# Strassen's algorithm for the first feed-forward product of seven token blocks, with the second product's weights streamed from DRAM

## The chip, the cores and the metric

The kernel runs on one core of a Trainium2 chip. The metric is the device time of one execution in microseconds (us). The core has a matrix engine (TensorE, here PE, with its weight loads listed as PEld), an elementwise engine (VectorE, DVE), an activation engine (ScalarE, ACT), a general engine (GpSimd, POOL), and SyncE (SP), which here only issues DMA transfers. Each engine works off its own instructions in order and waits on semaphores for the others. Matmuls write to PSUM, eight banks of 512 floats on each of 128 partitions; everything else lies in SBUF or in DRAM.

## The reference

Three stages run one after the other on 4608 tokens of 512 features: attention with pooled keys and values, a mixture of eight experts with one expert chosen per token, and a dense feed-forward stage with 2048 hidden features. The change concerns the last one:

```python
def _moe2_ref(x, w_in, w_out) -> np.ndarray:
    h = x @ w_in
    g = h * (1.0 / (1.0 + np.exp(-h)))
    return (g @ w_out).astype(np.float32)
```

x is 4608x512, w_in 512x2048, w_out 2048x512. The weights arrive as 64-bit floats.

## The kernel before

To keep the precision of float32, the kernel splits each operand of a large product into a high and a low part (`split`: ACT rounds the high part, DVE subtracts it) and adds three products, high x high, high x low and low x high.

The feed-forward stage (`ffn`) cuts the tokens into nine blocks of 512 (`ORDER`, last block first) and the hidden features into 16 blocks f of 128. A block's x is loaded (`load_x`), transposed on PE in four groups k of four 128x128 tiles (`xtrans`) and split into `xth` and `xtl`. The transposes go alternately to the PSUM tags "fxp" (one bank) and "hp" (three banks). For each f, `mm1` makes the first product, 12 matmuls of 512 columns (three split products x four slices of the 512 features) into one bank of "hp". ACT takes its sigmoid (`fsg`), DVE multiplies, ACT casts the high part (`fgh`), and DVE subtracts it (`fgl`). `mm2` makes the second product of f-1 meanwhile: 12 matmuls of 512 columns, which add onto four banks `fop0` to `fop3`, one for each 128 tokens of the block. So PE has mm1(f), mm2(f-1), mm1(f+1) and so on, and at a block's end mm2(15) with the next block's transposes between. `store` then copies the four banks out, the even ones on DVE and the odd ones on ACT, and SP sends them to DRAM.

The 16 weight pairs stay in SBUF all the time. They are converted from 64-bit floats (`ffn_ops`, `ffn_conv3`, steps taken from the generator `conv` inside `mm1`) while the first two blocks run. For that the first block is run in two visits, f 0 to 5 first and f 6 to 15 after the second block; the partial sums go to DRAM (`part`) between them and come back with `load_part`. So there are three visits, and then seven blocks that have nothing to convert.

All instructions of an engine keep the order in which the program writes them (`Ordered`): a copy that is written behind the steps of `conv` waits for them. The recorded line of almost every instruction is that helper's (L110), so the profile is read by tile names.

Of the kernel before, what the change touches and what calls it, by code (L numbers as in the profile page):

```python
# [5 lines left out]
F32 = mybir.dt.float32  # L6
F32R = mybir.dt.float32r
# [5 lines left out]
AF = mybir.ActivationFunctionType  # L13
ALU = mybir.AluOpType
# [4 lines left out]
P = 128  # L19
B, H, S, D = 8, 8, 576, 64  # L20
G = 72
NT = B * S
DM = H * D
# [129 lines left out]
class Kern:  # L153
# [931 lines left out]
    def ffn(self, xa, pool, dr):  # L1085
        nc, tc = self.nc, self.tc
        with tc.tile_pool(name="fs", bufs=1) as s1, \
# [61 lines left out]
            def store(b, ops, fs):  # L1149
# [9 lines left out]
                for s in range(4):  # L1159
                    o = s2.tile([P, DM], F32, name=f"fo{b}_{s}", tag="fo", bufs=4)  # L1160
                    if fs[0] > 0:
                        nc.vector.tensor_tensor(o, ops[s], self.part[s // 2][:, DM * (s % 2):DM * (s % 2 + 1)], ALU.add)
                    elif s % 2:
                        nc.scalar.copy(o, ops[s])
                    else:
                        nc.vector.tensor_copy(o, ops[s])
                    for bt, off, r, m in parts(4 * b + s):
                        nc.sync.dma_start(self.out[S * bt + off:S * bt + off + m, :], o[r:r + m, :])

            def load_part():  # L1170
                self.part = []
                for i in range(2):
                    t = mt[i]
                    nc.sync.dma_start(t.rearrange("p (s d) -> p s d", s=2),
                                      part[2 * i:2 * i + 2].rearrange("s p d -> p s d"))
                    self.part.append(t)


            self.ready = []

# [8 lines left out]
            def part_done(n):  # L1189
                if n + 1 < 16:  # L1190
                    self.ffn_abs(n + 1, *mt)
                self.ffn_conv3(n, pool)
                if n + 3 < 16:
                    self.ffn_load(n + 3)

            mt = [s1.tile([P, 2 * DM], F32, name=m, tag=m) for m in ("fm", "ft")]
            self.ffn_abs(NPRE, *mt)
# [5 lines left out]
            visits += [(b, range(16)) for b in ORDER[2:]]  # L1203
            for (b, fs), after in zip(visits, [v[0] for v in visits[1:]] + [None]):
                ops = [po.tile([P, DM], F32, name=f"fop{b}_{fs[0]}_{s}", tag=f"fop{s}") for s in range(4)]
                g = {}
                for f in fs:
                    g[f] = mm1(b, f, pace.pop(0) if pace else 2)
                    if f == fs[0] + 2 and after is not None:
                        load_x(after)  # L1210
                    if f == fs[0] + 4 and fs[0] > 0:
                        load_part()
                    if f == fs[-1] and after is not None:
                        xtrans(after, 0)
                        xtrans(after, 1)
                    if f > fs[0]:
                        mm2(f - 1, g.pop(f - 1), ops, fs)
                mm2(fs[-1], g.pop(fs[-1]), ops, fs, (lambda k: xtrans(after, k)) if after is not None else None)
                store(b, ops, fs)


def layout(q, k, v, w_skip, w_gate):
# [67 lines left out]
```

## Time and profile before

| | |
|---|---|
| median of 3 runs | 1363.56 us (1360.55 to 1364.36) |
| the profiled execution | 1363.74 us, its span 1362.0 us |
| PE busy | 1301.8 us, 96% of the span |
| PEld busy | 1111.8 us, 82% |
| DVE busy | 684.5 us, 50% |
| ACT busy | 502.9 us, 37% |
| POOL busy | 247.8 us, 18% |
| granted TensorE clock, mean | 0.987 |

The span runs from the first to the last instruction; 1.74 us of the execution lie around it. A group of instructions in the profile is named by what it writes and reads: "fh<-w1l,fh" is a matmul of the first product, "fop<-fh,fgh" one of the second. In a timeline each line has the start, the length of the whole run of equal instructions, and their number; what the engine waited for stands in brackets. A matmul's modelled end lies behind the next one's start, since matmuls overlap, so its pitch is read from starts.

### The profile page before, as it was taken

How to read it: one execution, taken by the hardware profiler on the slowest of the kernel's cores; microseconds unless marked ns; L12 is line 12 of the kernel's file. 1: busy time of each engine (PE TensorE's matmuls, PEld its weight loads, DVE VectorE, ACT ScalarE, POOL GpSimd, SP SyncE). 2: the span in 40 equal slices, each digit the busy share in tenths (PEclk: the TensorE clock that was granted, in tenths of full speed). 3: DMA queues.
4: the chain of work that ended last, by engine and by line, in shares of the span. 5: the costliest groups of instructions: out<-in, count | busy, mean ns of one | idle time of the engine just before them, and what ended most of it. 6: DMA issues, size and time to landing. Idle time of an engine off the chain costs nothing.

```text
span 1362.0 us, 19973 instructions
## 1 busy us (share of the span) xinstructions
PE 1301.8 (96%) x6645; PEld 1111.8 (82%) x6646; DVE 684.5 (50%) x1297; ACT 502.9 (37%) x1087; POOL 247.8 (18%) x216
## 2 busy tenths in 40 slices
PE   6899798999989998989999999999999999999998
PEld 5788687889978888878888888888888888888887
DVE  5777786766677766878523223232232232322322
ACT  4676534444455434354422223222232222322322
POOL 4466433322333431223200000000000000000000
PEclk9999998999989998999999999999999999999999
DMA  9998445555566542435021001001010010100000
GB/s 286 291 276 279 156 129 203 191 190 171 169 215 194 183 148 86 144 121 174 11 93 62 2 1 62 0 28 35 0 62 1 0 63 0 62 1 0 32 0 31
DMA packets 62997, 141.45 MB, mean 104 GB/s; under 512 B 11612, under 2 KB 21468, under 8 KB 60295
## 3 DMA queue, kind: packets, MB, share of 16 engines
q1 hardware_dynamic: 55631, 123.53, 28.0%
q0 software_dynamic: 7008, 16.80, 3.8%
q8 instruction: 43, 0.70, 0.2%
q10 hardware_dynamic: 288, 0.20, 0.1%
q14 instruction: 27, 0.22, 0.1%
HBM read 113.37 MB, written 29.82 MB: 105 GB/s over the span
## 4 chain that ended last, share of the span: by engine, by line
PE 58%; DVE 2%; issue 1%; ACT 0%; DVEq 0%; ACTq 0%
PE fop L110 28%; PE fh L110 28%; PE hp L110 1%; PE fxp L110 1%; DVE fr L110 1%; DVE ft L110 1%; PE yp L110 0%; DVE w1l L110 0%; ACT fm L110 0%; DVE fsg L110 0%; DVE fgl L110 0%; DVE raw L110 0%; ACT fh L110 0%; ACT fsg L110 0%; DVE x L110 0%
## 5 line engine op out<-in xcount | busy, mean ns | idle before, releaser
L110 DVE TENSOR_TENSOR fsg<-fh,fsg 128x512 f32<-128x512 f32 x144 | 99.6, 691 | 399.9 <-ACT fsg L110 399.9
L110 PE MATMUL fh<-w1l,fh 128*128 128x512 f32 x1008 | 248.9, 389 | 0.0
L110 ACT ACTIVATE fsg<-fh 128x512 f32<-128x512 f32 x144 | 86.3, 599 | 421.7 <-PE fh L110 421.6
L110 PEld LDWEIGHTS fh<-w1l,fh 128*128 128x128 f32 x1008 | 189.2, 188 | 39.5 <-DVE w1l L110 0.2
L110 PE MATMUL fop<-fh,fgh 128*128 128x512 f32 x504 | 199.2, 395 | 0.2 <-ACT fgh L110 0.2
L110 PE MATMUL fop<-fl,fgh 128*128 128x512 f32 x504 | 196.7, 390 | 0.0
L110 DVE TENSOR_TENSOR fgl<-fsg,fgh 128x512 fp32r<-128x512 f32 x144 | 99.7, 692 | 87.7 <-ACT fgh L110 87.4
L110 PE MATMUL fop<-fh,fgl 128*128 128x512 f32 x504 | 140.2, 390 | 1.6 <-DVE fgl L110 1.6
L110 ACT CAST fgh<-fsg 128x512 fp32r<-128x512 f32 x144 | 89.3, 620 | 123.4 <-DVE fsg L110 120.5
L110 PE MATMUL fh<-w1l,fl 128*128 128x512 f32 x504 | 134.7, 389 | 0.0
L110 PEld LDWEIGHTS fop<-fh,fgl 128*128 128x128 f32 x504 | 94.9, 188 | 21.9 <-DVE fgl L110 2.0
L110 PEld LDWEIGHTS fop<-fh,fgh 128*128 128x128 f32 x504 | 95.0, 189 | 19.3 <-ACT fgh L110 0.6
L110 PEld LDWEIGHTS fh<-w1l,fl 128*128 128x128 f32 x504 | 94.6, 188 | 19.6
L110 PEld LDWEIGHTS fop<-fl,fgh 128*128 128x128 f32 x504 | 95.0, 189 | 18.7
L110 PE MATMUL yp<-w2h,hh 128*128 128x512 f32 x240 | 96.8, 403 | 1.7 <-ACT w2h L110 1.7
L110 PE MATMUL yp<-w2l,hh 128*128 128x512 f32 x240 | 94.3, 393 | 2.2 <-DVE w2l L110 2.2
L110 PE MATMUL yp<-w2h,hl 128*128 128x512 f32 x240 | 94.7, 395 | 0.0
L110 ACT ACTIVATE hh<-hp 128x256 fp32r<-128x256 f32 (+2 forms) x96 | 41.2, 429 | 126.5 <-PE hp L110 119.6
L110 PE MATMUL hp<-xth,w1h 128*128 128x256 f32 (+2 forms) x384 | 73.7, 315 | 9.8 <-ACTq L943 5.9
L110 PE MATMUL hp<-xtl,w1h 128*128 128x256 f32 (+2 forms) x384 | 74.7, 313 | 7.2 <-DVE xtl L110 6.8
L110 ACT ACTIVATE prb<-s,mx 128x72 f32<-128x72 f32 x288 | 65.4, 344 | 43.2 <-DVE mx L110 43.2
L110 PE MATMUL hp<-xth,w1l 128*128 128x256 f32 (+2 forms) x384 | 71.7, 310 | 0.0
(181 smaller groups left out, 1885.9 us busy)
## 6 DMA issues: line engine op xcount, KB each, us to landing
raw<-w SPq DMA_DIRECT2D x88, 512.0 KB, 4.4
xa<-x SPq DMA_DIRECT2D x36, 256.0 KB, 5.0
fx<-xa SPq DMA_DIRECT2D x9, 1024.0 KB, 6.4
v<-vR SPq DMA_DIRECT2D x7, 1200.0 KB, 14.5
fr<-w_in SPq DMA_DIRECT2D x16, 512.0 KB, 4.4
fr<-w_out SPq DMA_DIRECT2D x16, 512.0 KB, 5.1
out<-fo SPq DMA_DIRECT2D x32, 256.0 KB, 2.4
k<-kT SPq DMA_DIRECT2D x7, 1152.0 KB, 10.0
```

What stands on the lines that cost most here:

```text
L110: ins = f(*a, **k)
```

## The change

The first two blocks stay as they are, in three visits. For the other seven, the first product is taken two hidden blocks at a time (a pair p, eight of them, called a slot here): x and the pair's 512x256 weights are both cut into 2x2 halves, and Strassen's algorithm in Winograd's form makes seven products of halves instead of eight. Each is three split products x two slices, so 42 matmuls of 256 columns a pair where there were 24 of 512. The seven products need sums of the halves of x (`xsum`, on DVE, from transposes `xt`, which ACT copies to SBUF), split like x, and sums of the halves of the weights. The latter are made once, by the generator `sums`, in the third visit (`SUMS` steps an f) and in the first slots of the first Strassen block. They overwrite the second product's weights in SBUF. Those were written to DRAM before (`keep_out`, on SP's queue) and are now streamed back for every block (`load_out`, on POOL's queue) into four buffers, used in turn.

A slot makes its products in four groups (`prods`), each into one bank of "hp": p1 and p6, p7 and p5, p4, p2 and p3. After each group stands a quarter of the second product of the slot before (`prev`, six matmuls). ACT and DVE combine the products into the pair's two results `c1` and `c0`, which then pass through the same sigmoid, product and split. `mid` holds what belongs to the change of block: `xsplit` at p=7 and p=0, `xt` at p=2, 3 and (two in a row) 4, `xsum` at p=5 and 6, and the two halves of `store` at the end of p=0 and in p=1.

```diff
+SUMS = [9] * 7 + [1] * 3
...
+            def keep_out(f):
+
+                for i, w in enumerate(self.fw[f]):
+                    nc.sync.dma_start(wout[f, i], w[:, 1].bitcast(F32))
...
             def load_part():
                 self.part = []
-                for i in range(2):
-                    t = mt[i]
-                    nc.sync.dma_start(t.rearrange("p (s d) -> p s d", s=2),
-                                      part[2 * i:2 * i + 2].rearrange("s p d -> p s d"))
+                for s in range(4):
+                    t = s2.tile([P, DM], F32, name=f"fp{s}", tag="fo", bufs=4)
+                    nc.sync.dma_start(t, part[s])
                     self.part.append(t)
...
                 self.ffn_conv3(n, pool)
                 if n + 3 < 16:
                     self.ffn_load(n + 3)
+                keep_out(n)
...
+            def sums():
...
+                    for o, n in ((3, w["11"]), (1, (h1, l1)), (0, w["22"])):
+                        op(q[o], *n, ALU.add)
+                        yield
+                    for o, a, b, do in ((0, q[0], q[1], ALU.add), (1, q[3], q[1], ALU.subtract), (2, q[0], q[3], ALU.subtract),
+                                        (3, *w["12"], ALU.add), (3, q[3], q[2], ALU.subtract)):
+                        op(q[o], a, b, do)
+                        if a.dtype == F32:
+                            nc.scalar.copy((h1, h3, h2, h4)[o], q[o])
+                        yield
+                    for o, (h, l) in enumerate(((h1, l1), (h3, l3), (h2, l2), (h4, l4))):
+                        op(l, q[o], h, ALU.subtract)
+                        yield
...
+            def xt(b, k):
+                ps = pp.tile([P, 512], F32, name=f"fxt{b}_{k}", tag="fxp")
+                for s in range(4):
+                    nc.tensor.transpose(ps[:, P * s:P * (s + 1)], xs[b][:, s, P * k:P * (k + 1)], self.ident)
+                nc.scalar.copy(self.xT[:, k], ps)
...
+            def load_out(i):
+
+                f, j = (i ^ 1) % 16, i % 4
+                t = [self.fw[4 * j + 1][1], self.fw[4 * j + 3][1]]
+                for k in range(2):
+                    nc.gpsimd.dma_start(t[k][:, 1], wout[f, k].bitcast(F32R))
+                stream[i] = t
+
+            def slot(b, p, prev, mid, tail=False):
...
+                def prods(*names):
+                    ps = self.hp.tile([P, 512], F32, name=f"fa{b}_{p}_{names[0][0]}", tag="hp")
+                    for j, (wn, xn) in enumerate(names):
+                        for i, (m, n) in enumerate(((0, 0), (0, 1), (1, 0))):
+                            for k in range(2):
+                                nc.tensor.matmul(half(ps, j), w[wn][m][:, P * k:P * (k + 1)], x[xn][n][:, k],
+                                                 start=(i == 0 and k == 0), stop=(i == 2 and k == 1))
+                    return [half(ps, j) for j in range(len(names))]
+
+                p1, u2, u3 = [snap[:, i] for i in range(3)]
+                p1_, p6 = prods(("11", "11"), ("S2", "T2"))
+                nc.scalar.copy(p1, p1_)
+                v.tensor_tensor(u2, p6, p1, ALU.add)
+                mid(0)
+                prev(0)
+                p7, p5 = prods(("S3", "T3"), ("S1", "T1"))
+                v.tensor_tensor(u3, p7, u2, ALU.add)
+                v.tensor_tensor(half(c1, 1), p5, u3, ALU.add)
+                v.tensor_tensor(u2, p5, u2, ALU.add)
+                mid(1)
+                prev(1)
+                p4, = prods(("22", "T4"))
+                v.tensor_tensor(half(c1, 0), p4, u3, ALU.add)
+                if not tail:
+                    prev(2)
...
+                nc.scalar.activation(sg[0], c1, AF.Sigmoid)
+                v.tensor_tensor(sg[0], c1, sg[0], ALU.mult)
+                nc.scalar.copy(gh[0], sg[0])
+                p2, p3 = prods(("12", "21"), ("S4", "22"))
+                v.tensor_tensor(half(c0, 0), p2, p1, ALU.add)
+                v.tensor_tensor(gl[0], sg[0], gh[0].bitcast(F32), ALU.subtract)
+                v.tensor_tensor(half(c0, 1), p3, u2, ALU.add)
+                if tail:
+                    prev(2)
+                prev(3)
+                nc.scalar.activation(sg[1], c0, AF.Sigmoid)
+                v.tensor_tensor(sg[1], c0, sg[1], ALU.mult)
+                mid(2)
+                nc.scalar.copy(gh[1], sg[1])
+                v.tensor_tensor(gl[1], sg[1], gh[1].bitcast(F32), ALU.subtract)
+                return list(zip(gh, gl))
...
-                    g[f] = mm1(b, f, pace.pop(0) if pace else 2)
...
+                    g[f] = mm1(b, f, pace.pop(0) if pace else 2 if after is not None else SUMS[f - HALF])
...
+                    if after is None:
+                        if f - HALF in (5, 6):
+                            xt(nb, 2 * (f - HALF) - 10)
+                            xt(nb, 2 * (f - HALF) - 9)
...
                     if f > fs[0]:
                         mm2(f - 1, g.pop(f - 1), ops, fs)
...
+                    def mid(i):
+                        if i == 0:
+                            if p == 1:
+                                store(*done, (2, 3))
+                            if p == 1 and nxt is not None:
+                                load_x(nxt)
+                            if p == 0:
+                                xsplit(b, "T4", "21", "22")
+                            if p == 7 and nxt is not None:
+                                xsplit(nxt, "11", "T2")
+                            if n == 0:
+                                for _ in range(3 if p == 0 else 7):
+                                    next(conv, None)
+                        if i == 1 and nxt is not None:
+                            if p in (2, 3):
+                                xt(nxt, p - 2)
+                            if p == 4:
+                                xt(nxt, 2)
+                                xt(nxt, 3)
...
+                            if p == 7:
+                                xsplit(nxt, "T3", "T1")
+                        if i == 2 and p == 0:
+                            store(*done, (0, 1))
+
+                    g2 = slot(b, p, prev, mid, p == 7 and nxt is None)
+                    prev = second(g2, fresh, 16 * n + 2 * p, p == 0, p == 7, count)
```

## Rows read from the trace of the kernel before

**Rows 1.** The page: busy time, share of the span and instructions of each engine, and the granted clock in 40 slices of the span.

```profile
PE 1301.8 (96%) x6645; PEld 1111.8 (82%) x6646; DVE 684.5 (50%) x1297; ACT 502.9 (37%) x1087; POOL 247.8 (18%) x216
...
PEclk9999998999989998999999999999999999999999
```

**Rows 2.** Stretches of the feed-forward stage: the bounds, their length, then busy us (and instructions) of PE, PEld, DVE, ACT and POOL, the granted clock, the DMA share and GB/s. The first is two plain blocks, the second the visit of the second block, the third the third visit.

```profile
908.01:1085.75 177.74, 177.74 (x802) 147.38 (x801) 51.88 (x76) 45.45 (x76) 0.00 (x0) 1.00 0.07 24
...
592.42:681.31 88.89, 88.89 (x401) 73.70 (x400) 64.83 (x69) 40.27 (x55) 25.32 (x10) 1.00 0.28 95
681.31:737.54 56.23, 56.23 (x257) 46.66 (x256) 17.63 (x27) 14.93 (x25) 0.00 (x0) 1.00 0.16 57
```

**Rows 3.** The longest waits between 592 and 1362 us, of all engines (us in total, times, longest us); the list has no row of PE or PEld.

```profile
ACT fsg L110 <- PE fh L110: 418.9, 135, 3.8
DVE fsg L110 <- ACT fsg L110: 397.4, 133, 3.7
```

**Rows 4.** Groups of instructions by shape, whole span: busy us, mean ns of one, then idle time before them.

```profile
L110 ACT CAST w1l<-fxp 128x512 fp32r<-128x512 f32 x40 | 22.3, 587 | 30.7 <-PE fxp L110 30.7
...
L110 DVE SCALAR_TENSOR_TENSOR hl<-hp,hh 128x256 fp32r<-128x256 f32 x40 | 17.0, 425 | 10.9 <-ACT hh L110 10.2 <-ACT w2h L110 0.6
...
L110 ACT ACTIVATE hh<-hp 128x256 fp32r<-128x256 f32 x40 | 15.4, 385 | 43.0 <-PE hp L110 40.5 <-PE xtp L110 2.5
...
L110 DVE COPY fo<-fop 128x512 f32<-128x512 f32 x16 | 10.3, 681 | 1.3 <-PE fop L110 1.3
```

**Rows 5.** PE's timeline: the end of a 512-column group and the 256-column matmuls that follow, 24 lines of four (96 matmuls) up to the transposes at 288.58; then a plain slot of a later block, 12 matmuls of 512 columns from 904.38 to 907.10, and the second product's start at 902.57 behind a first product.

```profile
277.05 0.39 PE L110 MATMUL yp<-w2h,hl 128*128 128x512 f32 x1
277.27 0.63 PE L110 MATMUL hp<-xth,w1h 128*128 128x256 f32 x4
...
288.58 0.82 PE L110 MATMUL xtp<-ident,xn 128*128 128x128 f32 x6
...
902.57 0.39 PE L110 MATMUL fop<-fh,fgh 128*128 128x512 f32 x1
...
904.38 1.07 PE L110 MATMUL fop<-fh,fgl 128*128 128x512 f32 x4
905.29 1.98 PE L110 MATMUL fh<-w1l,fh 128*128 128x512 f32 x8
907.10 1.07 PE L110 MATMUL fh<-w1l,fl 128*128 128x512 f32 x4
```

**Rows 6.** PE's timeline in another iteration of the same stage: the first matmuls after a pause, and later ones, 24 matmuls from 220.75 to the start at 223.47.

```profile
216.41 1.33 PE L110 MATMUL hp<-xth,w1h 128*128 128x256 f32 x4 [5.89 <-ACTq L943]
...
220.75 0.62 PE L110 MATMUL hp<-xth,w1h 128*128 128x256 f32 x4
...
223.47 0.62 PE L110 MATMUL hp<-xth,w1h 128*128 128x256 f32 x4
```

**Rows 7.** PE's timeline: eight transposes of 128 columns and the matmul behind them.

```profile
908.01 1.03 PE L110 MATMUL fxp<-ident,fx 128*128 128x128 f32 x8
908.80 0.48 PE L110 MATMUL fop<-fh,fgh 128*128 128x512 f32 x1
```

**Rows 8.** The timeline of ACT and DVE behind one first product: sigmoid, product, cast, subtraction.

```profile
902.83 0.60 ACT L110 ACTIVATE fsg<-fh 128x512 f32<-128x512 f32 x1 [3.46 <-PE fh L110]
...
903.46 0.69 DVE L110 TENSOR_TENSOR fsg<-fh,fsg 128x512 f32<-128x512 f32 x1 [3.37 <-ACT fsg L110]
...
904.18 0.62 ACT L110 CAST fgh<-fsg 128x512 fp32r<-128x512 f32 x1 [0.76 <-DVE fsg L110]
...
904.84 0.69 DVE L110 TENSOR_TENSOR fgl<-fsg,fgh 128x512 fp32r<-128x512 f32 x1 [0.69 <-ACT fgh L110]
```

**Rows 9.** DVE's timeline: two small operations, the second of which reads the first one's result, and two larger ones that don't read each other's.

```profile
536.48 0.17 DVE L110 TENSOR_SCALAR gt<-gt 128x3 f32<-128x3 f32 x1
536.68 0.18 DVE L110 RECIPROCAL gt<-gt 128x3 f32<-128x3 f32 x1
...
579.16 0.69 DVE L110 TENSOR_TENSOR fgl<-fsg,fgh 128x512 fp32r<-128x512 f32 x1
579.77 1.22 DVE L110 SCALAR_TENSOR_TENSOR ft<-fr,ft 128x1024 uint32<-128x1024 uint32 x1
```

**Rows 10.** PE's timeline at the end of the first visit: the transposes that waited for a split, and the first and last of the slow stretch behind them (six matmuls of 512 columns and four transposes between the starts at 588.26 and 591.71); then a pause of another stage and matmuls some time behind it.

```profile
587.80 0.81 PE L110 MATMUL fxp<-ident,fx 128*128 128x128 f32 x4 [1.84 <-DVE w1l L110]
588.26 0.78 PE L110 MATMUL fop<-fh,fgh 128*128 128x512 f32 x1
...
591.71 0.40 PE L110 MATMUL fop<-fh,fgh 128*128 128x512 f32 x1
...
395.81 0.82 PE L110 MATMUL hp<-xtl,w1h 128*128 128x256 f32 x2 [3.42 <-DVE xtl L110]
...
397.70 1.05 PE L110 MATMUL hp<-xtl,w1h 128*128 128x256 f32 x4
```

**Rows 11.** The DMA issues (number, KB each, median us from issue to landing), POOL's timeline at one indirect issue and DVE's beside it.

```profile
fr<-w_out SPq DMA_DIRECT2D x16, 512.0 KB, 5.1
...
540.95 0.98 POOL L110 DMA_INDIRECT xa<-x,sq  x1 [18.73 <-ACT w1l L110]
...
540.49 1.29 DVE L110 TENSOR_TENSOR w1l<-fxp,w1l 128x512 fp32r<-128x512 f32 x2 [0.30 <-ACT w1l L110]
```

More of the change, by code (lines that the diff above doesn't have):

```diff
@@ L1158, in store @@
                     return
-                for s in range(4):
-                    o = s2.tile([P, DM], F32, name=f"fo{b}_{s}", tag="fo", bufs=4)
+                for s in ss:
+                    o = None if fs[0] > 0 else s2.tile([P, DM], F32, name=f"fo{b}_{s}", tag="fo", bufs=4)
                     if fs[0] > 0:
-                        nc.vector.tensor_tensor(o, ops[s], self.part[s // 2][:, DM * (s % 2):DM * (s % 2 + 1)], ALU.add)
+                        o = self.part[s]
+                        nc.vector.tensor_tensor(o, ops[s], o, ALU.add)
                     elif s % 2:
@@ new lines, in xsum, with xsplit @@
+            def xsum(b, n):
+                x, y = {"T1": ("12", "11"), "T2": ("22", "T1"), "T3": ("22", "12"), "T4": ("21", "T2")}[n]
+                nc.vector.tensor_tensor(xv(n, b), xv(x, b), xv(y, b), ALU.subtract)
+            def xsplit(b, *names):
+                for n in names:
+                    self.split(*self.xo[n], xv(n, b))
+            stream = {}
+            def load_out(i):
[4 more added lines that the diff above has]
+                stream[i] = t
@@ new lines, in second, with quarter @@
+            def second(g, ops, i, first, last, count):
+                def quarter(q):
+                    t, ss = q // 2, (2 * (q % 2), 2 * (q % 2) + 1)
+                    gh, gl = g[t]
+                    h, l = [w[:, 1] for w in stream[i + t]]
+                    for s in ss:
+                        m = slice(P * s, P * (s + 1))
+                        nc.tensor.matmul(ops[s], gh[:, m], h, start=(first and t == 0), stop=False)
+                        nc.tensor.matmul(ops[s], gh[:, m], l, start=False, stop=False)
+                    for s in ss:
+                        nc.tensor.matmul(ops[s], gl[:, P * s:P * (s + 1)], h, start=False, stop=(last and t == 1))
+                    if q % 2 and i + t + 4 < count:
+                        load_out(i + t + 4)
+                return quarter
@@ L1202, in ffn @@
             visits = [(ORDER[0], range(HALF)), (ORDER[1], range(16)), (ORDER[0], range(HALF, 16))]
-            visits += [(b, range(16)) for b in ORDER[2:]]
-            for (b, fs), after in zip(visits, [v[0] for v in visits[1:]] + [None]):
+            for f in range(NPRE):
+                keep_out(f)
+            nb = ORDER[2]
+            for (b, fs), after in zip(visits, (ORDER[1], ORDER[0], None)):
                 ops = [po.tile([P, DM], F32, name=f"fop{b}_{fs[0]}_{s}", tag=f"fop{s}") for s in range(4)]
+                if after is None:
+                    for _ in conv:
+                        pass
+                    while self.ready:
+                        self.ready.pop(0)()
+                    conv = sums()
+                    tokens()
                 g = {}
                 for f in fs:
-                    g[f] = mm1(b, f, pace.pop(0) if pace else 2)
-                    if f == fs[0] + 2 and after is not None:
-                        load_x(after)
+                    g[f] = mm1(b, f, pace.pop(0) if pace else 2 if after is not None else SUMS[f - HALF])
+                    if f == fs[0] + 2:
+                        load_x(nb if after is None else after)
                     if f == fs[0] + 4 and fs[0] > 0:
@@ L1216, in ffn @@
                     if f > fs[0]:
                         mm2(f - 1, g.pop(f - 1), ops, fs)
-                mm2(fs[-1], g.pop(fs[-1]), ops, fs, (lambda k: xtrans(after, k)) if after is not None else None)
-                store(b, ops, fs)
+                if after is not None:
+                    mm2(fs[-1], g.pop(fs[-1]), ops, fs, lambda k: xtrans(after, k))
+                    store(b, ops, fs)
+            blocks = ORDER[2:]
+            count = 16 * len(blocks)
+            prev, done = None, (b, ops, fs)
@@ new lines, in ffn, with prev @@
+            for n, b in enumerate(blocks):
+                nxt = blocks[n + 1] if n + 1 < len(blocks) else None
+                fresh = [po.tile([P, DM], F32, name=f"fop{b}_{s}", tag=f"fop{s}") for s in range(4)]
+                for p in range(8):
+                    if prev is None:
+                        gh, gl = g.pop(15)
+                        h, l = self.fw[15]
+                        def prev(s, ops=ops):
+                            m = slice(P * s, P * (s + 1))
+                            for i, (x, w) in enumerate(((gh, h), (gh, l), (gl, h))):
+                                nc.tensor.matmul(ops[s], x[:, m], w[:, 1], start=False, stop=(i == 2))
+                            if s == 3:
+                                load_out(3)
+                    def mid(i):
[17 more added lines that the diff above has]
+                                xt(nxt, 3)
+                            if p == 5:
+                                xsum(nxt, "T1")
+                                xsum(nxt, "T3")
+                            if p == 6:
+                                xsum(nxt, "T2")
+                                xsum(nxt, "T4")
+                            if p == 7:
[4 more added lines that the diff above has]
+                    prev = second(g2, fresh, 16 * n + 2 * p, p == 0, p == 7, count)
+                done = b, fresh, range(16)
@@ L1222, in layout @@
+            for q in range(4):
+                prev(q)
+                if q > 1:
+                    store(*done, (2 * q - 4, 2 * q - 3))
 def layout(q, k, v, w_skip, w_gate):
```

52 lines of the change are left out of this document (51 added, 1 removed).

## The prediction

> **What bounds the kernel now.** I read the page first: TensorE (PE) is busy 96% of the span and nearly always at the upper of its two clock levels [rows 1]. Then the stretches: after 592 us PE is busy for the whole of each, at a granted clock of 1.00, while VectorE (DVE) and ScalarE (ACT) are under a third busy in the plain blocks [rows 2]. The list of waits for 592 to 1362 us has no row of PE at all; its longest rows are ACT and DVE waiting for PE [rows 3]. So the nine blocks are a pure stream of matmuls, and each matmul less is worth its pitch, as long as nothing new makes PE wait. Two blocks take 177.74 us [rows 2], one 88.87: 384 matmuls of 512 columns at 0.2267 us (12 of them, 4 and 8, start in 2.72 us [rows 5]) are 87.05, and the 16 transposes with their switches 1.8.
>
> **The change part by part.**
>
> *Matmuls.* For each pair of hidden blocks the first product has 7 products x 3 x 2 = 42 matmuls of 256 columns instead of 24 of 512. The mixture-of-experts stage has the same form, a fresh 128x128 weight each: 96 of them, coming straight from 512-column ones without a pause, start between 277.27 and 288.58 us [rows 5], 0.1178 us each. 42 x 0.1178 = 4.95 against 24 x 0.2267 = 5.44: 0.49 less, and over 8 pairs x 7 blocks **-27.6 us**. The same form also runs quicker: after a pause, 24 start in 2.72 us, 0.1133 each [rows 6]; that would give -38.1. I take 0.1178, because the new groups of 12 follow 512-column groups without a pause.
> The Trainium skill (TensorE: Matmul & The Clock Gate, Back-to-back issue gap) puts the gap at N/2.4 + 2.5 ns, 109 and 216 ns; an estimate by it is 0.595 us a pair, -33.3 in all and a sum of 1361. Both rows lie above it, by 9 and 11 ns, and by either a fixed part per matmul speaks against 42 matmuls for 24; the rows decide.
>
> *Second product.* Same 24 matmuls a pair, in quarters of six (1.36 us) set between the products. Its weights come from DRAM on POOL's queue, two of 256 KB per hidden block, four hidden blocks ahead: a load issued after one slot's quarter is read two slots later, some 16 us. Loads of 512 KB land in 5.1 us [rows 11]. I cost them at nothing; they would cost the excess if one took over 16 us. The copies to DRAM (keep_out) join SP's queue behind ffn_load; in the first change of block the load of x gets two issues in front of it and comes about 1 us later, where PE waits over 3 us for DVE anyway [rows 10]: nothing, at most 1 us.
>
> *A steady slot.* PE: 42 x 0.1178 + 24 x 0.2267 = 10.39 us. A 256-column DVE operation takes 0.425 [rows 4]; back to back, operations start about 0.08 before the last one's end (0.69 long, next start after 0.61), but 0.03 behind it if they read its result [rows 9]. A slot has 7 of these and 4 of 512 columns. Count from the slot's start, and let a consumer start 0.26 after the last pitch of the whole bank's products (the activation at 902.83 against a product ending at 902.57 [rows 5, 8]). Then c1 is complete at 6.97, sigmoid, product and cast as in [rows 8] bring its hi part at 8.97 and its lo part at 10.3; c0 is complete at 10.66, its hi at 12.67, its lo at 13.4. PE wants the first at 11.8 and the second at 16.6. No wait; a slot is PE's.
> Every reader of a product in the rows starts after its bank's last matmul, so I let them here too; if one may start when its half of the bank is done, c0 comes 0.7 earlier. The Trainium skill (PSUM — Partial Sum Buffer, PSUM bank collisions raise a hardware error) says to guard by bank and not by address, which would give the later time; no trace here shows a bank that is read in halves.
>
> *Change of block.* The splits of p=7 and p=0 (0.61 each on DVE) fit into the gaps before p5 and p4, so the c0 chain keeps its times. In slot p=0 the copies of fop0 and fop1 stand behind the second product with the sigmoid (12.02). fop0's copy (0.68) ends at 12.62, and PE wants that bank for the next slot's first quarter at 11.8: 0.85 us of wait, or 0.1 with the half-bank reading. Six times 0.85: **+5.1**.
>
> *Transposes.* xt has one bank, where xtrans alternated between two. At p=4 two stand in a row: the second waits for modelled end (0.27) + 0.1 + ACT's copy 0.587 [rows 4] of the first. That is **+0.92** in each of six blocks, 5.5. The transposes themselves, 0.79 us for eight [rows 7], stay 16 a block.
>
> *The weight sums in the third visit.* Each f now carries nine steps of 256 columns on DVE, with up to four copies on ACT. From one sigmoid to the next ACT and DVE need sigmoid 0.60, product 0.69, cast 0.62, gl 0.61 [rows 8, 9], eight steps at 0.34 to 0.46 (2.9), some 5.5, against PE's 5.44; and the visit's first two products come 2.72 apart, so they start late and stay late: 0.5 us of wait at f=8, and at f=11 the sigmoid starts 2.4 us after its product.
> There xt(0) and xt(1) follow at once. xt(1) needs xt(0)'s bank, whose copy stands in ACT's order behind sigmoid, cast and the copies of the nine steps: 2.4 + 0.60 + 0.72 + 0.65 + 0.65 + 2.9 + 0.5 + 0.6 is 9.1 us after the product, less 0.4 of transposes: **8.7**. At f=12 the lag is gone and the only copy is in the second step: 0.26 + 0.60 + 0.72 + 0.65 + 0.65 + 0.42 + 0.43 + 0.65, 4.4, less 0.4: **4.0**. Together +13.2. The kernel shows this kind of wait today: at 587.80 the transposes waited 1.84 for a split behind conversion steps on DVE [rows 10].
> After that pause the clock was half: six matmuls and four transposes took from 588.26 to 591.71 [rows 10], 3.45 us instead of 1.8. I add 1.6 for each of the two long pauses: **+3.2**.
>
> *First Strassen block.* Its slot p=0 carries only f=15's second product (7.67 us), yet DVE has in it three splits, three sum steps, 11 own operations and two additions of the saved part. In sequence, fop0 is free at 12.3 after the slot's start; PE wants it at 9.1: 3.2, and 0.15 more for fop1. After a pause of 3.42 at 395.81 the clock fell for a while too, later and in part [rows 10], so half of 1.6 comes on top: **+4.2**.
>
> *Sum.* -27.6 + 5.1 + 5.5 + 13.2 + 3.2 + 4.2 = +3.6. The profiled execution took 1363.74 (span 1362.0 and 1.74 around it), 0.18 over the median of the runs; so 1363.74 + 3.6 - 0.2 = **1367 us**. A saving of 2% is handed back, two thirds of it in one visit.
>
> **The rivals.**
> 1. *The quick pitch.* The 256-column groups run at 0.1133: -10.5 on the sum, 1357. For it: the 24 of [rows 6]; against it: they began after a pause at the low clock, and those after 512-column groups did not.
> 2. *The third visit doesn't wait.* If ACT takes xt's copy ahead of the steps' copies, 16.4 go: 1351. For it: two stalls so plain would be easy to avoid; against it: in the trace splits keep their written place behind conversions [rows 10].
> 3. *Slower: POOL holds DVE back.* POOL now issues four streamed loads a slot. If DVE stands still for each issue, about 1.0 us as POOL's indirect one took [rows 11], two of them fall into the c0 chain that ends with fop0's copy: 2 us more at each of six changes of block, which have no slack, so 1367 + 12 = 1379. Ordinary slots have 3.2 spare (16.6 - 13.4) and hide it. It decides from the first tenth at a change of block, and in every slot from 3.2. Against it: the two splits beside POOL's issue at 540.95 took 1.29 together [rows 11], as much as 0.61 + 0.69.
> 4. *The change doesn't do what it says*, and PE has as many columns as before: the diff excludes it, 42 x 256 against 24 x 512 can be counted.
>
> **How the numbers follow.** A difference under 0.3%, 4 us, can hardly be told from none here: faster is below 1359.5, slower above 1367.6. My forecast has 0.47, with a range of its own of 1361 to 1374 (half-bank start -4.5 below; DVE without overlap, 3 more in the visit, and a third loss of clock above): 0.03 faster, 0.22 within, 0.22 slower. The quick pitch has 0.18 (0.15 faster, 0.03 within), no wait in the visit 0.15 (faster), POOL or another hindrance on DVE 0.20 (slower). Sum: 0.33, 0.25, 0.42. The range reaches to both outer cases, 1350 to 1379.
>
> **What would show it.** Matmuls: 256-column starts 118 ns apart, 1008 more matmuls in all. Visit: PE rows "fxp" waiting for ACT xT twice, near 8.7 and 4.0 us, both followed by a window of lower granted clock. Blocks: a period near 86.7 us (84.9 and two waits of 0.9) instead of 88.87, with PE waits on "fop" for the copies "fo" and on "fxp" for xT, six of each. The prediction is wrong if PE has no wait over 3 us between 680 and 760, if a plain slot is not close to 10.4 us, or if the streamed weights appear among PE's waits.

## The result and the profile after

The changed kernel takes 1377.01 us (median of 4 runs, 1375.18 to 1381.26) against 1362.29 us for the kernel before on the same chip: a ratio of 1.0112 [1.0083, 1.0141], some 15 us slower. The forecast was 1367 us. Slower had the largest of the three chances, but the price is 15 us where the sum said 3.6. The time lies outside the forecast's own range of 1361 to 1374; only the whole range of 1350 to 1379, which reached that far for another reason, has it.

The page of the kernel after, its first lines and two lines of the DMA issues, which answer to [rows 1] and [rows 11]:

```profile
span 1373.2 us, 23359 instructions
PE 1288.9 (94%) x7653; PEld 1141.9 (83%) x7654; DVE 889.8 (65%) x1834; ACT 560.3 (41%) x1224; POOL 367.9 (27%) x440
...
fl<-wout POOLq DMA_DIRECT2D x196, 256.0 KB, 3.0
...
w1h<-wout POOLq DMA_DIRECT2D x28, 256.0 KB, 3.1
```

PE has 7653 matmuls instead of 6645, the 1008 that the change adds by count. The two DMA lines are the streamed weights, 224 loads in all. For the first time in the blocks behind the first visit PE stands still. These are PE's waits from the first feed-forward product on, all but one of 0.3 us (us in total, times, longest us); between 592 and 1362 us the kernel before had none [rows 3], and ahead of that some 3.6 us:

```profile
PE fxt L111 <- ACT xT L111: 16.4, 8, 8.7
PE fop L111 <- ACT fgh L111: 9.1, 10, 3.0
PE fxp L111 <- DMA fx<-xa: 3.6, 1, 3.6
```

The name in the second row needs care. This is the wait at one change of block:

```profile
937.53 0.68 DVE L111 COPY fo<-fop 128x512 f32<-128x512 f32 x1
...
937.70 0.62 ACT L111 CAST fgh<-fsg 128x512 fp32r<-128x512 f32 x1 [0.34 <-DVE fsg L111]
...
938.31 0.47 PE L111 MATMUL fop<-fl,fgh 128*128 128x512 f32 x1 [0.73 <-ACT fgh L111]
```

The cast that PE's bracket names ends at 938.32, when PE has already started, so it can't be what PE waited for. DVE's copy of fop0 ends at 938.21, 0.10 us ahead of PE, and it does so at all six changes of block. In the first Strassen block DVE's addition of the saved part ends 0.10 ahead of PE in the same way. The other three of the ten, 1.8 us in all, lie in the visits and not at a change of block.

One period of a Strassen block, from a wait for fop to the next block's (columns as in [rows 2]): 88.11 us, where a plain block took 88.87 and the forecast had 86.7:

```profile
937.30:1025.41 88.11, 86.70 (x546) 78.05 (x545) 50.43 (x102) 29.36 (x54) 16.87 (x33) 1.00 0.41 120
```

The stage ahead of the feed-forward one starts its last work at different times in different executions (the first feed-forward product begins at 551.92 us before, at 547.74 after), so the two profiled executions are compared from that product on. From its start to the start of the last matmul PE takes 805.6 us before and 820.8 after. Summed over the starts of the trace, with the waits taken out:

| from the first feed-forward product | before | after | difference |
|---|---|---|---|
| matmuls of 512 and 256 columns | 788.1 | 775.0 | -13.1 |
| transposes | 14.0 | 16.2 | +2.2 |
| waits of PE | 3.6 | 29.5 | +25.9 |

A wait counts from the modelled end of the instruction ahead of it. What that one runs beyond its pitch stands in the first two rows: 0.24 us for four transposes (0.60 long, 0.36 from start to start), eight times, which is nearly all of their 2.2, and 0.16 for a product group (1.59 and 1.43).

So the waits took back twice what the matmuls saved. The forecast had 27.2 us of waits and 23.6 us of savings (27.6, less 4.0 for the clock). The waits came close to their price; some 10 us of the saving did not come.

Where the saving stayed away is seen in a plain slot of the kernel after, p1 of one slot to p1 of the next (PE's timeline, columns as in [rows 5]):

```profile
992.42 0.64 PE L111 MATMUL fa<-xc,fh 128*128 128x256 f32 x4
...
993.85 1.09 PE L111 MATMUL fop<-fl,fgh 128*128 128x512 f32 x4
...
995.24 0.88 PE L111 MATMUL fa_S<-xc,fl 128*128 128x256 f32 x6
...
1002.98 0.64 PE L111 MATMUL fa<-xc,fh 128*128 128x256 f32 x4
```

From 992.42 to 1002.98 are 10.56 us, not 10.39. Twelve 256-column matmuls take 1.43 us, 0.1193 each (the first of a group 0.113, the others 0.120), where 0.1178 was assumed. The six of the second product behind them take 1.39 us, where six took 1.36 before [rows 5]: their mean is 0.2313 instead of 0.2267, and the loss is in the first three of them (0.233, 0.236, 0.228, 0.233, 0.230, 0.227).

### The profile page after: what moved, and what is told of

Read it like the earlier page. It is cut to its first block, busy times and chain, and to the rows that moved or that the text cites. A ratio compares the mean times of both kernels' runs of the same rounds, so it can differ in the third digit from the quotient of the medians.

```text
span 1373.2 us, 23359 instructions
## 1 busy us (share of the span) xinstructions
PE 1288.9 (94%) x7653; PEld 1141.9 (83%) x7654; DVE 889.8 (65%) x1834; ACT 560.3 (41%) x1224; POOL 367.9 (27%) x440
## 4 chain that ended last, share of the span: by engine, by line
PE 54%; DVE 4%; ACT 2%; issue 1%; DMA 1%; POOL 0%; SPq 0%; ACTq 0%; DVEq 0%; POOLq 0%
PE fop L111 27%; PE fa L111 14%; PE fa_S L111 6%; PE fh L111 4%; PE hp L111 1%; DVE ft L111 1%; PE yp L111 1%; PE fxt L111 1%; DVE fsg L111 1%; ACT fgh L111 1%; DVE fgl L111 1%; DMA fx<-xa 1%; ACT fsg L111 1%; PE fxp L111 0%; DVE fm L111 0%
## 5 line engine op out<-in xcount | busy, mean ns | idle before, releaser
L111 PE MATMUL fop<-fl,fgh 128*128 128x512 f32 x896 | 274.8, 398 | 7.4 <-ACT fgh L111 7.4
L111 POOL DMA_DIRECT2D fl<-wout x196 | 103.4, 531 | 569.0 <-PE fop L111 541.4
L111 ACT ACTIVATE fsg<-fm 128x512 f32<-128x512 f32 x112 | 70.8, 632 | 270.4 <-DVE fm L111 270.4
L111 PE MATMUL fop<-fl,fgl 128*128 128x512 f32 x448 | 139.2, 392 | 0.0
L111 DVE TENSOR_TENSOR fsg<-fm,fsg 128x512 f32<-128x512 f32 x112 | 77.5, 692 | 84.8 <-ACT fsg L111 84.8
L111 DVE TENSOR_TENSOR fm<-fa,snap 128x256 f32<-128x256 f32 x168 | 70.7, 421 | 86.6 <-PE fa L111 86.6
L111 PE MATMUL fa<-xc,fh 128*128 128x256 f32 x686 | 105.6, 282 | 0.0
L111 PEld LDWEIGHTS fa<-xc,fh 128*128 128x128 f32 x686 | 98.7, 190 | 8.0
L111 PEld LDWEIGHTS fop<-fl,fgl 128*128 128x128 f32 x448 | 84.4, 188 | 19.4
L111 PE MATMUL fa<-w1l,fh 128*128 128x256 f32 x490 | 74.5, 283 | 0.0
```

Of the source, the lines that this page charges most:

```text
L111: ins = f(*a, **k)
```

## The experiments

Times and ratios are medians against the kernel before; "from the first product" is the profiled execution from the first feed-forward product to the end of the span, 810.05 us before and 825.5 after.

**Two banks for the transposes.** The transposes of xT alternate between "fxp" and "hp", as those of the kernel before did.

```diff
-                ps = pp.tile([P, 512], F32, name=f"fxt{b}_{k}", tag="fxp")
+                ps = (self.hp if k % 2 else pp).tile([P, 512], F32, name=f"fxt{b}_{k}", tag="hp" if k % 2 else "fxp")
```

> xt alternates between the PSUM tags fxp and hp, as xtrans did; the rest is the changed kernel (1377.0 us). Theory (transposes in a row wait for one bank's copy, and the clock falls after the long pause): the waits of fxt on ACT xT go (8.7 + 3.7 in the third visit, 0.68 in each of six blocks = 16.4 us) and with them the half-clock stretch behind the first (some 1.6 us), so 18 us less: about 1359, slightly under the kernel before. Rival (ACT and DVE are late in that visit anyway, and PE then waits for the sums or the splits a few us later): 5 to 10 us less, 1367 to 1372, and new waits of PE between 720 and 760 us.

Measured: 1359.33 us (10 runs), ratio 0.9981 [0.9957, 1.0006]; from the first product 807.4, which is 18.1 less than after. PE's timeline of this kernel at the two places:

```profile
705.21 1.03 PE L111 MATMUL fxt<-ident,fx 128*128 128x128 f32 x8
...
714.48 1.97 PE L111 MATMUL fxt<-ident,fx 128*128 128x128 f32 x8 [2.78 <-ACT xT L111]
```

At f=11 all eight transposes now run in one go; at f=12 the third finds the first one's bank not copied yet, because ACT is still behind. Of the 18.1 us, 14.3 are waits of PE, 1.7 transposes (what they ran past their pitch) and 2.1 the products. The single bank made 13.6 of the 16.4 us of waits for xT, as expected; with a second one the change costs nothing that these runs can tell from none, instead of 1.1%.

**No stream.** Only the first four loads of second-product weights are made; later pairs use the buffers as they are.

```diff
+                if i > 3:
+                    stream[i] = stream[i % 4]
+                    return
```

> Leaves out all streamed loads but the first four; the second product of later pairs uses the four buffers' old contents. Theory (the pitch is set by the change between 256 and 512 columns): pitches stay at 119.3 and 231.3 ns, a plain slot at 10.56 us, time as the changed kernel, 1377 within 2. Rival (streamed writes into SBUF slow PE's reads): pitches go back to 117.8 and 226.7, a slot to 10.39, 56 x 0.17 = 9.5 us less, 1367. Second rival (POOL's issues hold DVE back): the 0.73 us waits at the changes of block get shorter, up to 4 us less.

Measured: 1374.51 us (4 runs), ratio 1.0079 [1.0050, 1.0108], an interval that overlaps that of the changed kernel; from the first product 825.9 against 825.5. (This execution has a stretch of lower clock behind f=12, worth some 1.6 us, that the changed kernel's did not have.) POOL's busy time falls from 367.9 to 254.5 us as it must, and the slot does not get shorter (PE's timeline of this kernel):

```profile
995.96 0.64 PE L111 MATMUL fa<-xc,fh 128*128 128x256 f32 x4
...
997.39 1.09 PE L111 MATMUL fop<-fl,fgh 128*128 128x512 f32 x4
...
998.78 0.88 PE L111 MATMUL fa_S<-xc,fl 128*128 128x256 f32 x6
```

Again 1.43 and 1.39 us. A whole block of this kernel, between the same points as above, with the DMA engines' share at 0.07 instead of 0.41 (columns as in [rows 2]):

```profile
940.89:1028.99 88.10, 86.64 (x546) 78.02 (x545) 50.43 (x102) 29.35 (x54) 0.00 (x0) 1.00 0.07 25
```

It takes 88.10 us without streamed loads and 88.11 with them. Neither the transfers nor POOL's issues lengthen the pitch, and the waits at the changes of block do not get shorter (0.78 instead of 0.73). So a block costs the same with the stream and without it.

**Groups in pairs.** Two product groups, then two quarters of the second product, so that PE changes between the two shapes about half as often.

```diff
                 mid(0)
-                prev(0)
...
                 mid(1)
+                prev(0)
                 prev(1)
...
-                if not tail:
-                    prev(2)
...
-                if tail:
-                    prev(2)
+                prev(2)
                 prev(3)
```

> The slot's order is two product groups, two quarters of the second product, two groups, two quarters, so half as many changes between 256 and 512 columns. Theory (each change costs: six 512-column matmuls behind a change take 1387 ns instead of 1360): two changes less a slot, 0.05 us, 56 slots: 3 us less; and the next block's first quarter comes later, so the 0.73 us waits for fop go, 6 x 0.73 = 4.4 us, and part of the 2.97 of the first Strassen block: about 1367 to 1370. Rival (the pitch is that of the operands): pitches unchanged, only the 4.4 to 7 of the waits: 1370 to 1373. In both the 256-column pitch tells: 117 to 118 by the theory if the change sets it, 119 to 120 by the rival.

Measured: 1370.52 us (8 runs), ratio 1.0058 [1.0034, 1.0083], 6.5 less than after by the medians and 10.1 from the first product. PE's timeline of this kernel, two groups and two quarters:

```profile
946.54 0.88 PE L111 MATMUL fa<-w1l,fh 128*128 128x256 f32 x6
947.26 1.09 PE L111 MATMUL fop<-fl,fgh 128*128 128x512 f32 x4
...
948.65 1.07 PE L111 MATMUL fop<-fl,fgh 128*128 128x512 f32 x4
...
950.01 0.64 PE L111 MATMUL fa<-xc,fh 128*128 128x256 f32 x4
```

The first six still take 1.39 us, the second six 1.36: the excess of the 512-column matmuls belongs to each change of shape and halves with their number (mean 2.75/12 = 0.2292). That is worth 24 x 0.0021 x 56 = 2.8 us. The 256-column ones stay at 0.120 (946.54 to 947.26 for six): the part of the theory that had them fall to 117 to 118 is a miss. The rest of the gain is in waits: the six of 0.73 at the changes of block are gone, since the second product now asks for its first bank one product group later, and the 2.97 of the first Strassen block became 1.53 and 0.33 without a stretch of lower clock behind it. A wait of 1.2 us for a late load of x, and 1.3 more at one pair of transposes, came in exchange. The profiled execution was the fastest of the eight, 7.7 us under their median, so its 10.1 says too much; the median lies just inside the rival's range, and it is the pitches that decide for the theory.

**Wide products.** The 42 matmuls of 256 columns of a slot become 24 of 512, on the same groups; the groups' order, the copies and all other work stay.

```diff
-                    for j, (wn, xn) in enumerate(names):
-                        for i, (m, n) in enumerate(((0, 0), (0, 1), (1, 0))):
-                            for k in range(2):
-                                nc.tensor.matmul(half(ps, j), w[wn][m][:, P * k:P * (k + 1)], x[xn][n][:, k],
-                                                 start=(i == 0 and k == 0), stop=(i == 2 and k == 1))
+                    some = [(wn, xn, m, n, k) for wn, xn in names for m, n in ((0, 0), (0, 1), (1, 0)) for k in range(2)]
+                    some = some[:7 if len(names) > 1 else 3]
+                    for j, (wn, xn, m, n, k) in enumerate(some):
+                        nc.tensor.matmul(ps, w[wn][m][:, P * k:P * (k + 1)], x[xn][n].rearrange("p k n -> p (k n)"),
+                                         start=(j == 0), stop=(j == len(some) - 1))
```

> Leaves out Strassen's saving and nothing else: a slot's products are made of 24 matmuls of 512 columns (7, 7, 3 and 7) with the same weights and tokens in place of 42 of 256; the products' values are no longer the right ones. It measures what the seven products give by themselves. Theory (pitches of the profile: 42 x 0.1193 = 5.01 and the second product's 24 x 0.2313 = 5.55, against 48 x 0.2267 = 10.88 when every matmul has 512 columns): the changed kernel saves only 0.32 us a slot, so this one is 56 x 0.32 = 18 us slower, 1395, with pitches of 226 to 227 everywhere. Rival (the prediction's term, 0.49 a slot, with the loss elsewhere): 27.6 slower, 1405.

Measured: 1398.06 us (4 runs), ratio 1.0250 [1.0218, 1.0282]; 21.0 above after by the medians and 20.8 from the first product. A slot of it, start to start, from PE's timeline:

```profile
994.00 1.07 PE L111 MATMUL fa<-xc,fh 128*128 128x512 f32 x4
...
1000.57 1.07 PE L111 MATMUL fop<-fl,fgh 128*128 128x512 f32 x4
...
1001.93 1.07 PE L111 MATMUL fa<-xc,fh 128*128 128x512 f32 x4
...
1004.88 1.07 PE L111 MATMUL fa<-xc,fh 128*128 128x512 f32 x4
```

994.00 to 1004.88 is 10.88 us, 48 times 0.2267, and a quarter takes 1.36 again. With one shape alone the excess is gone from the second product. So Strassen's products save 10.88 - 10.56 = 0.32 us a slot, 17.9 us over 56 slots, and not 27.6; the other 2.9 us of the difference are nearly all in the 2.7 us lost to a stretch of lower clock after the wait at f=12 (5.8 us from 731.42 to 737.24, where 3.1 is normal), which the changed kernel's profiled execution did not have.

**Lighter sums.** The steps for the weight sums are spread, 6 an f and 4 in the last three instead of 9 and 1, with none in the first Strassen slot.

```diff
-SUMS = [9] * 7 + [1] * 3
+SUMS = [6] * 7 + [4] * 3
...
-                                for _ in range(3 if p == 0 else 7):
+                                for _ in range(0 if p == 0 else 7):
```

> The changed kernel with six weight-sum steps an f in the third visit (then four) in place of nine (then one), and none in the first Strassen slot. Theory (xt waits for its copy behind the steps of the same f, and ACT is late from the f before): the lag at f=11 goes, and the copies stand at other steps. At f=11 the only copy is in the second of six steps, so the wait is as at f=12 before, 3.7; at f=12 they are in the last three, so 0.26 + 0.60 + 0.72 + 0.65 + 0.65 + 1.9 + 1.0 less 0.4, near 5.1. Together 8.8 instead of 12.3, the first Strassen block's 2.97 falls by the three steps' 1.1, and the small wait of 0.35 goes: 5 us less than the changed kernel, about 1372. Rival (the wait at f=11 is the lag of the visit and not the order within the f): the wait falls below 2 us, and the kernel is 10 or more faster, 1367.

Measured: 1376.58 us (4 runs), ratio 1.0119 [1.0086, 1.0152], no gain. PE's timeline of this kernel at f=11 and f=12 and in the first Strassen block:

```profile
713.59 1.11 PE L111 MATMUL fxt<-ident,fx 128*128 128x128 f32 x4 [3.67 <-ACT xT L111]
...
726.87 1.10 PE L111 MATMUL fxt<-ident,fx 128*128 128x128 f32 x4 [5.26 <-ACT xT L111]
...
760.82 0.55 PE L111 MATMUL fop<-fl,fgh 128*128 128x512 f32 x1 [2.34 <-issue]
```

The two waits are as computed: they are set by the number of steps between the sigmoid and the copy of xT, and the lag that these steps build up. The total is a miss. The wait at f=12 now has a slow stretch behind it, and the steps that moved on lengthen waits in the first Strassen block (one at the two transposes in a row is 1.56 instead of 0.68, the next fop 1.59 instead of 0.73). It shifted the cost, as long as the bank was single.

**Two banks and pairs**, the first and the third edit together.

> Both xt's alternation of banks and the order of two product groups, two quarters. Theory (the two act at different places): the gains add, 18 + 10 less than the changed kernel, about 1349, 1.0% faster than before. Rival (the order by pairs shifts the time at which xt's copies and loads of x are wanted, and new waits come): 1352 to 1358.

Measured: 1351.55 us (4 runs), ratio 0.9920 [0.9898, 0.9942]. By the medians it is 25.5 us less than after, and the two edits alone gave 17.7 and 6.5: within the noise the gains add. From the first product it is 24 us, of 28.2 that the two gave alone, but there the second edit's 10.1 comes from its fastest execution. Its longest waits are the load of x (3.2), the transposes at f=12 (2.8) and 1.5 in the first Strassen block.

**All three edits**, with the lighter sums on top.

> The same with the lighter sums of e5. Theory: the 2.8 us that e1 still waited for xT at f=12 and the 0.35 go, and of the first Strassen block's 1.5 us the most; 4 to 5 us less than e6, about 1345. Rival (the load of x and the splits take the place as the last to come): as e6.

Measured: 1344.98 us (5 runs), ratio 0.9880 [0.9859, 0.9902]: faster than the kernel before by 1.2% and than the changed one by 32 us. Its three longest rows of PE's waits from the first product on, and its two double transposes of the third visit:

```profile
PE fxp L111 <- DMA fx<-xa: 2.8, 1, 2.8
PE fop L111 <- ACT fgh L111: 1.7, 3, 1.2
PE fa_S L111 <- ACT xc L111: 1.0, 1, 1.0
```

```profile
709.45 1.03 PE L111 MATMUL fxt<-ident,fx 128*128 128x128 f32 x8
...
715.78 1.04 PE L111 MATMUL fxt<-ident,fx 128*128 128x128 f32 x8
```

With the second bank in place, the lighter sums are worth 6.6 us by the medians: the 2.8 us at f=12 and the lower clock behind it are gone, and of the 2.7 in the first Strassen block 1.8 are left (1.0 and 0.2 for splits, 0.2 and 0.3 for fop). Alone they were worth nothing that the runs can tell from noise (0.4 us).

**One operand.** Every product matmul reads the same weight tile and the same slice of tokens.

```diff
-                                nc.tensor.matmul(half(ps, j), w[wn][m][:, P * k:P * (k + 1)], x[xn][n][:, k],
+                                nc.tensor.matmul(half(ps, j), w["11"][0][:, 0:P], x["11"][0][:, 0],
```

> Every matmul of the seven products reads the same weight tile and the same slice of the tokens; the rest as the changed kernel, so the products' values are not the right ones. It asks what sets the 256-column pitch of 119 to 120 ns, where the same form takes 117.8 in the experts' stage. If it is where the operands lie (reads of weights and tokens that meet in SBUF), the pitch changes, by 2 ns or more in either direction. If it is the form of the groups (a 256-column matmul whose weight load starts only with the matmul before it), it stays at 119 to 120 within 0.5, after a first one of 113.

Measured: 1379.01 us, one run. PE's timeline:

```profile
994.62 1.59 PE L111 MATMUL fa<-xc,fh 128*128 128x256 f32 x12
996.05 1.09 PE L111 MATMUL fop<-fl,fgh 128*128 128x512 f32 x4
...
997.44 1.59 PE L111 MATMUL fa_S<-xc,fh 128*128 128x256 f32 x12
```

1.43 and 1.39 as ever. So the place of the products' operands in SBUF, and whether they read the same ones again, have no part in the pitch.

## Why the prediction was right and wrong

*What bounds the kernel* was right: PE before and after, with each matmul worth its pitch and each wait coming on top.

*The range.* That it holds 1377 is luck. The forecast's own ended at 1374; above that stood only the rival in which POOL or something else holds DVE back, but the waits at the changes of block came out as priced and the kernel without the stream takes as long. The time is there because a part of the saving did not come that the forecast did not doubt.

*Matmuls, -27.6: the step that failed.* The sign and the mechanism were right, the size was not. The pitch of 0.1178 came from another stage, where 256-column matmuls follow each other in a long row, and the second product was held at 0.2267 as if its neighbours did not matter. In the blocks they are 0.1193 and 0.2313. The first costs 42 x 0.0015 x 56 = 3.5 us, the second 24 x 0.0046 x 56 = 6.2 us, so -17.9 was the value of this term. The half that was not looked at ("Same 24 matmuls a pair") lost more than the half that was computed. What makes the 512-column ones slower is the change of shape: their excess halves with half the changes and is gone with none. The forecast's own sign, a plain slot of 10.4 us, shows it: 10.56. The experiment with wide products gives the 17.9 from the other side.
By the N/2.4 + 2.5 ns of the Trainium skill (TensorE: Matmul & The Clock Gate, Back-to-back issue gap), which it gives for a matmul by itself, these would be 109 and 216 ns; the runs lie 10 and 15 ns above it, further than [rows 5] did.

*Second product and its stream, nothing:* right for the stream. The 224 loads land in some 3 us, PE never waits for one, and without them nothing is gained. The copies to DRAM were put at no more than 1 us, hidden behind a wait for DVE. Here is the place, PE's and SP's timeline, first of the kernel before and then of the kernel after:

```profile
571.46 0.38 SPq L110 DMA_DIRECT2D fx<-xa  x1
...
579.16 1.04 PE L110 MATMUL fxp<-ident,fx 128*128 128x128 f32 x8
...
585.46 0.49 PE L110 MATMUL fop<-fh,fgl 128*128 128x512 f32 x1 [1.58 <-DVE fgl L110]
```

```profile
570.00 0.47 SPq L111 DMA_DIRECT2D fx<-xa  x1
...
579.66 1.65 PE L111 MATMUL fxp<-ident,fx 128*128 128x128 f32 x8 [3.62 <-DMA fx<-xa]
...
585.67 0.60 PE L111 MATMUL fxp<-ident,fx 128*128 128x128 f32 x4
```

The load of x is now waited for, 3.62 us, and the waits of 1.58 and of 1.84 [rows 10] behind it are gone, presumably because DVE caught up while PE stood. So the sum was near zero by luck and not for the reason given: the late load came ahead of the waits and replaced them. The load was also later than the "about 1 us" of the forecast. Counted from the first product it is issued 2.7 us later (at 22.3 us instead of 19.5), of which the two copies in front of it take 0.9; and PE can start only 9.7 us behind the issue, where 7.7 were enough before. That the copies cause all of this was not tried by itself.

*Change of block, +5.1:* six waits of 0.73 and 0.16 of run-out each, 0.89 and 5.3 in all, for DVE's copy of fop0 as said. Right, and with the whole bank's end (0.85 was predicted) rather than the half's (0.1). DVE's first read of p7 in the slot shown above starts like this:

```profile
996.87 0.42 DVE L111 TENSOR_TENSOR snap<-fa_S,snap 128x256 f32<-128x256 f32 x1 [1.07 <-PE fa_S L111]
```

p7's own six matmuls end at 996.11, the bank's twelve at 996.83. That is what the Trainium skill's advice to guard by bank (PSUM — Partial Sum Buffer, PSUM bank collisions raise a hardware error) would give; the traces agree.

*Transposes, +5.5:* six waits like this one, and 0.24 of run-out:

```profile
975.03 0.66 PE L111 MATMUL fxt<-ident,fx 128*128 128x128 f32 x4 [0.68 <-ACT xT L111]
```

That is 0.92 each, as predicted, though the three terms that the forecast lists for it add up to 0.96.

*The sums in the third visit, +13.2:* right in place and size. In the kernel after, PE, and ACT's order that makes it wait:

```profile
707.52 0.60 PE L111 MATMUL fxt<-ident,fx 128*128 128x128 f32 x4
716.78 1.12 PE L111 MATMUL fxt<-ident,fx 128*128 128x128 f32 x4 [8.66 <-ACT xT L111]
717.55 0.78 PE L111 MATMUL fop<-fh,fgh 128*128 128x512 f32 x1
...
728.54 0.66 PE L111 MATMUL fxt<-ident,fx 128*128 128x128 f32 x4 [3.67 <-ACT xT L111]
```

```profile
710.06 0.59 ACT L111 ACTIVATE fsg<-fh 128x512 f32<-128x512 f32 x1
711.40 0.62 ACT L111 CAST fgh<-fsg 128x512 fp32r<-128x512 f32 x1 [0.76 <-DVE fsg L111]
715.10 0.41 ACT L111 CAST fh<-ft 128x256 fp32r<-128x256 f32 x1 [3.07 <-DVE ft L111]
...
715.84 0.40 ACT L111 CAST fh<-ft 128x256 fp32r<-128x256 f32 x1
716.15 0.58 ACT L111 COPY xT<-fxt 128x512 f32<-128x512 f32 x1
```

The first four transposes are done at 707.9, and the sigmoid starts 2.5 us behind its product's last pitch, where 2.4 was computed. Then ACT takes the cast and three copies of the sums in their written order, with 3.07 us of waiting for DVE among them, before the copy of xT that PE needs. It waits 8.66 us (8.7 predicted; the terms listed for it add up to 8.6), then 3.67 (4.0), and 0.36 at f=8 (0.5).

*The clock, +3.2 and 0.8:* the kernel after, in stretches of 10 us (columns as in [rows 2]):

```profile
710.00:720.00 10.00, 3.22 (x10) 2.74 (x11) 4.72 (x12) 3.48 (x8) 0.00 (x0) 0.66 0.00 0
720.00:730.00 10.00, 6.33 (x33) 5.09 (x32) 4.46 (x11) 2.69 (x5) 0.00 (x0) 1.00 0.00 0
...
760.00:770.00 10.00, 9.56 (x49) 8.41 (x50) 7.79 (x18) 2.37 (x5) 1.05 (x2) 0.83 0.76 245
```

After the wait of 8.66 the clock was at the lower of its two levels (1.2 instead of 2.4 GHz) until about 720: four transposes and six matmuls took 3.36 us (716.78 to 720.14) where 1.75 is normal, 1.6 lost. After the 3.67 at f=12 there was no loss in this execution; in three of the four experiments with the same wait of 3.67 there the clock did fall. After the 2.97 of the first Strassen block it was some 1.7, twice the 0.8 expected. Together 3.3 against 4.0.

*First Strassen block, 3.35 of waiting:* 2.97 and 0.16, for DVE's addition out of fop0 as said. 1.4 us of waits in the second block's visit, near 621 and 628 us, had no term.

*The rivals.* The quick pitch of 0.1133 is there, but for the first matmul of a group alone. The third visit without a wait and POOL holding DVE back are excluded, the first by the waits above, the second by the kernel without a stream. Of the 11.6 us between forecast and measurement on this stretch (3.6 and 15.2), 9.7 are the pitch and 1.4 the waits that had no term.

## What to carry to other kernels

A pitch is a property of a sequence and not of an instruction: when groups of another shape are put between matmuls that themselves stay, time a short mixed sequence on the chip, and count a loss on both kinds. Where a sum of terms of both signs comes out near zero, as here, an error of 0.17 us in a slot of 10.4 is larger than the sum.

When a step is moved onto a PSUM tag with a single bank, look up in the written order what stands between its two writers on the engine that empties it. Here that was one copy behind nine steps of other work, and a second bank gave back 18.1 us, as much as the algorithm saved.

Edits that act on the same wait need not add: lighter sums gave nothing that could be measured alone and 6.6 us once the bank was doubled, while the second bank and the pairs, which act at different places, did add.

Check the name that a wait is put down to against the times: an instruction that ends after the waiting one has started did not release it.

## What the runs showed of the hardware

A 512-column matmul group directly behind 256-column ones starts slower: six take 1.39 us instead of 1.36, some 0.027 us for each change of shape, and a second six right behind them take 1.36 again. With one shape only, as in the kernel with wide products, 0.2267 holds over a whole slot.

256-column matmuls between such groups keep 0.120 us from the third one on (the first is 0.113), with their own operands or all with the same, and with or without transfers running beside them; in the experts' stage of the same execution they keep 0.1178. What makes this difference of 2 ns stays open.

224 loads of 256 KB issued by POOL, with the DMA engines busy for 0.41 of a block instead of 0.07, left PE's pitch unchanged in the third digit: 1.43 and 1.39 us a group with the stream and without it.
